# A gated mix of a long convolution and a token MLP: constant transform tables, rows in eights, one more butterfly, and a work order written out as a list

## The chip, the cores and the metric

The kernel runs on one core of a Trainium2 chip. The core has a matrix engine (TensorE, PE in the profile; its weight loads stand as PEld), VectorE (DVE), ScalarE (ACT), GpSimd (POOL) and SyncE (SP), which here only issues DMA transfers. Each engine works through its own queue in order and waits on semaphores. The metric is the device time of one execution in microseconds.

## What is computed

```python
def _A_ref(q, k, v, shift_k, ssm_k, ssm_D):        # q, k, v: [1, 2048, 640]
    k_shift = zeros; for t in range(4):
        k_shift += k_pad[:, t:t + S, :] * shift_k[:, 3 - t]
    kv = k_shift * v
    kv_f = rfft2(kv padded to 4096); kf_f = rfft2(ssm_k padded to 4096)
    y = irfft2(kv_f * kf_f)[:, :S, :].astype(bfloat16)
    return q * (y + kv * ssm_D)

def _B_ref(x, w1, b1, w2, b2):                     # over the tokens
    h = _layernorm(x)                              # over the 640 channels
    u = gelu(einsum("bsd,sf->bdf", h, w1) + b1)    # F = 1536
    return (einsum("bdf,fs->bds", u, w2) + b2).transpose(0, 2, 1)

x = A_q
g = sigmoid((x * gate_w).sum(-1, keepdims=True))
return g * _A_ref(x, ...) + (1 - g) * _B_ref(x, ...)
```

All inputs are bfloat16; S = 2048 tokens, D = 640 channels.

## The kernel before

Everything is held in on-chip memory once loaded. Tokens lie on the 128 partitions, channels along the free axis, in halves of 320 columns per matmul.

**Two strands.** The MLP strand: X (A_q) is loaded in four groups of 512 rows; per tile of 128 tokens VectorE takes `bn_stats` twice and `bn_aggr` once (`ln_tile`), GpSimd makes the reciprocal root (`ln_scale`), VectorE normalises X in place (`ln_apply`). Then 12 x 4 groups of eight matmuls ("m1", X by the w1 chunks in `ring`) with a gelu on ScalarE, and 16 output tiles of 24 matmuls ("m2", GT by W2), each with an eviction on ScalarE into O1. The convolution strand: the ssm kernel is transposed on TensorE (`transp`, tile wT), transformed with cosine and sine tables (`fwd`, `fwd_even`, table FTB, result C), and combined by additions on VectorE (`mixing`); k is reordered (`k_turn`, on VectorE), transposed by DMA, convolved with the four taps on TensorE (`kv`) and multiplied by v; the two halves of kv go through the same transforms; `cross` and `product` multiply the spectra on VectorE, with some sums left to accumulating DMAs from GpSimd's queue; `invmix` makes the additions of the inverse transform, and `inverse` does its matmuls, scales them by the gate on ScalarE ("cg"), multiplies by q and adds to O1 on VectorE, and writes the output. Half 0 of the sequence goes first, half 1 last.

**Tables.** The 4096-point transform is split into four phases p = 0..3 (the rows 4i + p). The table FTB is made in the kernel: GpSimd writes index patterns (`iota` into brow, acol, jrow), VectorE makes index products modulo 4096 (pint), and ScalarE takes the sine, four times. The inverse's table is FTB transposed by four DMA transposes into GTB, then reordered by four ScalarE copies back into FTB ("gil").

**Even phases.** The forward transforms of phases 0 and 2 use half the matmuls and three VectorE additions (`fwd_even`) for all but the first half of the ssm kernel. The inverse uses eight matmuls per output tile for every phase.

**Start.** TensorE runs matmuls on a tile of zeros (`spin`) until the first data is there and between the transposes of ssm: `SPIN = (7, 2, 1, 1, 1)`, and one more ahead of the first transform. SyncE's queue loads ssm block 0, ssm blocks 1 and 2, x0, ssm blocks 3 and 4, x1, x2, x3, the biases, the second half of ssm, w1 and k, in that order.

**What sets the order.** Every step is added once to a planner (`SC.add`, class `_Sched`), with an engine, an estimated duration, what it reads and writes, and a priority. `run` plays these through a model with one queue per engine, four PSUM slots and a DMA model, and emits each engine's instructions in the order found. A tracker (`_Tracker`) then puts the semaphore waits in. Matmul accumulators are taken from four slots of two banks (pp0 to pp3).

```python
SPIN = (7, 2, 1, 1, 1)
LB = [0, 8, 13, 16]                       # tiles per batch of the layernorm's roots
W2S = ((20, 24, 28), (16, 0, 4), (8, 12, 20), (24, 28, 16))
```

Of the kernel before, what the change touches and what calls it, by code (L numbers as in the profile page):

```python
# [313 lines left out]
class _Op:  # L314
    __slots__ = ("eng", "dur", "emit", "prio", "idx", "ndep", "succ", "vt", "vtrole", "end", "start", "kind", "lat", "deps", "name", "after", "nafter", "asucc", "lock")
# [13 lines left out]
class _Sched:  # L329
# [29 lines left out]
    def add(self, eng, dur, emit, reads, writes, prio=None, vt=None, lat=0.0, name=""):  # L359
# [9 lines left out]
        if vt is not None:  # L369
            vt.left += 1  # L370
            if vt.last_pe is not None:
                deps.add(vt.last_pe)
            if eng == "PE":
                if vt.first is None:
                    vt.first = op
                vt.last_pe = op
            else:
                for d in deps:
                    if d.vt is not vt and not vt.keep:
                        if d not in vt.first.deps:  # L380
                            vt.first.deps.add(d)
        op.deps = deps
        op.after = set()
        self._rec(op, reads, "R")
# [4 lines left out]
    def run(self):  # L389
        ops = self.ops  # L390
        for op in ops:
            op.succ = []
            op.asucc = []
            op.ndep = len(op.deps) + len(op.after)
        for op in ops:
            for d in op.deps:
                d.succ.append(op)
            for d in op.after:
                d.asucc.append(op)
        engs = list(ENGS) + ["SP", "QA"]  # L400
        ready = {e: [] for e in engs}
        pend = {e: [] for e in engs}
        free = {"ACT": 2.93, "DVE": 0.85, "POOL": 0.83, "PE": 1.18, "SP": 0.0, "QA": 0.0}
        port = {"DVE": 0.0, "POOL": 0.0}
        dma_free = 0.3
        avail = {}
        for op in ops:
            avail[op] = 0.0
            if op.ndep == 0:
                heapq.heappush(pend[op.eng], (0.0, op.prio, op.idx))  # L410
        nfree = list(range(self.NSLOT))
        held = {}
        events = []
        order = []
        t = 0.0
        done = 0
        started = 0
        n = len(ops)
        frees = []
        while started < n:  # L420
            while frees and frees[0][0] <= t:
                _, sl, cls = heapq.heappop(frees)
                nfree.append(sl)
                held[cls] -= 1
            nxt = []
            progress = False
            for e in engs:
                while pend[e] and pend[e][0][0] <= t:
                    _, p, i = heapq.heappop(pend[e])
                    heapq.heappush(ready[e], (p, i))  # L430
                if free[e] > t:
                    nxt.append(free[e])
                    continue
                skipped = []
                pick = None
                while ready[e]:
                    p, i = heapq.heappop(ready[e])
                    op = ops[i]
                    if op.vt is not None and op.vt.slot is None:
                        c = op.vt.cls  # L440
                        if not nfree or held.get(c, 0) >= self.limit.get(c, 99):
                            skipped.append((p, i))
                            continue
                    pick = op
                    break
                for s in skipped:
                    heapq.heappush(ready[e], s)
                if pick is None:
                    if pend[e]:
                        nxt.append(pend[e][0][0])  # L450
                    continue
                op = pick
                progress = True
                started += 1
                if op.vt is not None and op.vt.slot is None:
                    op.vt.slot = nfree.pop(0)
                    held[op.vt.cls] = held.get(op.vt.cls, 0) + 1
                op.start = t
                if e in ("SP", "QA") or op.lat < 0:
                    issue = 1.2 if e == "POOL" else 0.1  # L460
                    s = max(t + issue, dma_free)
                    dma_free = s + op.dur
                    op.end = dma_free + 2.0 + (6.0 if e == "POOL" else 0.0)
                    free[e] = t + issue
                else:
                    op.end = t + op.dur
                    if op.lock:
                        op.end += max(port["POOL" if e == "DVE" else "DVE"] - t, 0.0)
                        port[e] = op.end
                    free[e] = op.end  # L470
                order.append(op)
                if op.vt is not None:
                    op.vt.left -= 1
                    if op.vt.left == 0:
                        heapq.heappush(frees, (op.end + 0.05, op.vt.slot, op.vt.cls))
                for s in op.asucc:
                    avail[s] = max(avail[s], op.start)
                    s.ndep -= 1
                    if s.ndep == 0:
                        heapq.heappush(pend[s.eng], (avail[s], s.prio, s.idx))  # L480
                for s in op.succ:
                    lat = 0.08 if s.eng == e else 0.15
                    if e == "PE" and s.eng == "PE":
                        lat = 0.0
                    avail[s] = max(avail[s], op.end + lat)
                    s.ndep -= 1
                    if s.ndep == 0:
                        heapq.heappush(pend[s.eng], (avail[s], s.prio, s.idx))
                nxt.append(free[e])
            if not progress:  # L490
                c = [x for x in nxt if x > t]
                if frees:
                    c.append(frees[0][0])
                assert c, "schedule stuck: " + str([(o.name, o.eng, o.ndep) for o in ops if not hasattr(o, "end")][:12])
                t = min(c)
        self.order = order
        self.makespan = max(o.end for o in ops)
        return order
# [6 lines left out]
def bass_gated_mix__ssm_conv_h3__mixer_token_mlp__prompt_kernel(  # L505
    nc, A_q, A_k, A_v, A_shift_k, A_ssm_k, A_ssm_D, B_x, B_w1, B_b1, B_w2, B_b2, gate_w, out
):
    with nc.Block() as blk:

        @blk.tensor  # L510
        def _(pe_engine):
            _build(nc, A_q, A_k, A_v, A_shift_k, A_ssm_k, A_ssm_D, B_x, B_w1, B_b1, B_w2, B_b2, gate_w, out)


def _build(nc, A_q, A_k, A_v, A_shift_k, A_ssm_k, A_ssm_D, B_x, B_w1, B_b1, B_w2, B_b2, gate_w, out):
# [10 lines left out]
    with ExitStack() as es:  # L526
# [48 lines left out]
        gth = alloc("gth", [128, 16], F32)  # L575
# [4 lines left out]
        FTB = alloc("FTB", [128, 4, 2, 2, 2, 128], BF16)  # L580
        GTB = alloc("GTB", [128, 4, 2, 2, 2, 128], BF16)
# [6 lines left out]
        acol = alloc("acol", [128, 1], I32, at=base_of(SS))  # L588
        brow = alloc("brow", [128, 128], I32, at=base_of(SS) + 64)
        prod = alloc("prod", [128, 128], I32, at=base_of(SS) + 64 + 2048)  # L590
        tb = alloc("tb", [128, 2, 2, 128], I16, at=base_of(SS) + 64 + 2560)
# [13 lines left out]
        pint = alloc("pint", [128, 4, 2, 2, 256], I16, at=base_of(ring[1]))  # L605
        jrow = alloc("jrow", [128, 8, 256], I16, at=base_of(ring[1]) + 8192)
# [7 lines left out]
        cgb = [alloc(f"cgb{i}", [128, 2, D], BF16, at=base_of(GTB) + 2560 * i) for i in range(3)]  # L614
# [7 lines left out]
        def dve_dur(n, mode):  # L622
            return n / {1: 960.0, 2: 1920.0, 4: 3840.0}[mode] + (0.04 if mode == 4 else 0.08)

        def act_dur(n, nap=0):
            return n / 1200.0 + 0.09 + 0.05 * nap
# [32 lines left out]
        def act(o, i, func, bias=None, scale=None, acc=None, vt=None, prio=None, name="act"):  # L659
# [17 lines left out]
            return SC.add("ACT", act_dur(n_of(o), nap), emit, rr if vt is not None else rr + [i], ww, prio=prio, vt=vt, name=name)  # L677
# [21 lines left out]
        def mms(vt, items, prio=None, name="mm"):  # L699
            dur = sum(max(n_of(r) / 2400.0 + 0.0025, 0.056) for _, _, r, _, _ in items)  # L700
# [11 lines left out]
        last = [None]  # L712

        def dma(o, i, nbytes, stream="SP", prio=None, sem=None, rate=365.0, chain=False, **kw):
# [7 lines left out]
            if chain:  # L722
                if last[0] is not None:
                    o_.after.add(last[0])
                last[0] = o_
# [14 lines left out]
        def ssm_load(h, a, b):  # L740
            dma(ssm[:, a:b, 1024 * h:1024 * h + 1024], dr(A_ssm_k, 128 * S * a + 1024 * h, [[S, 128], [128 * S, b - a], [1, 1024]]), 128 * (b - a) * 2048, chain=True, rate=({0: 262.0, 1: 223.0}.get(a, RL3)) if h == 0 else 385.0)
# [625 lines left out]
```

## Time and profile before

Three runs took 179.3, 179.79 and 182.12 us, median 179.79. One further execution was profiled; the profile gives its span, 178.7 us from the first instruction to the last, and not its own time.

| engine or queue | busy us | what it does most |
|---|---|---|
| PE | 170.9 | 1104 matmuls of 320 columns, 160 of the taps, 80 transposes |
| DVE | 169.5 | additions and products of the transforms |
| ACT | 117.0 | 64 evictions into C (40.5), 15 into O1 (13.3), 16 of the inverse (12.7) |
| POOL | 43.1 | KF (8.1), index patterns, issue of accumulating DMAs |
| DMA | 43.51 MB | mean 243 GB/s over the span |

The profile's page lists the busy time of each engine, the idle time just before groups of instructions with what ended it, and a chain of waits followed back from the last instruction. A table by stage gives the same busy times for stretches of the span. Rows of the timeline give the start, the length, the engine, the source line, the operation and how many were merged. A row "x3" of several instructions overlaps a little: the start-to-start time of one is a bit below its duration. Line 298 is the helper that issues every matmul, 632 that of every two-input VectorE or GpSimd operation, 676 that of every ScalarE operation, 272 that of every DMA.

### The profile page before, as it was taken

How to read it: one execution, taken by the hardware profiler on the slowest of the kernel's cores; microseconds unless marked ns; L12 is line 12 of the kernel's file. 1: busy time of each engine (PE TensorE's matmuls, PEld its weight loads, DVE VectorE, ACT ScalarE, POOL GpSimd, SP SyncE). 2: the span in 40 equal slices, each digit the busy share in tenths (PEclk: the TensorE clock that was granted, in tenths of full speed). 3: DMA queues.
4: the chain of work that ended last, by engine and by line, in shares of the span. 5: the costliest groups of instructions: out<-in, count | busy, mean ns of one | idle time of the engine just before them, and what ended most of it. 6: DMA issues, size and time to landing. Idle time of an engine off the chain costs nothing.

```text
span 178.7 us, 3326 instructions
## 1 busy us (share of the span) xinstructions
PE 170.9 (96%) x1373; PEld 128.4 (72%) x1374; DVE 169.5 (95%) x203; ACT 117.0 (65%) x176; POOL 43.1 (24%) x52
## 2 busy tenths in 40 slices
PE   7868999899999999999999999999999999999993
PEld 2545787487778677776777778888888887777772
DVE  7799889979999999999999899999999999999984
ACT  4998997999899999428999921131231323753760
POOL 8099803100000065000241100403525000252000
PEclk9999999999999999999999999999999999999999
DMA  5999999999999999999499989797999999599463
GB/s 145 384 413 372 388 301 206 264 421 299 213 258 289 189 272 235 229 229 231 97 244 285 173 132 363 158 229 241 171 194 221 208 201 394 205 164 236 114 233 138
DMA packets 38542, 43.51 MB, mean 243 GB/s; under 512 B 15867, under 2 KB 31360, under 8 KB 38528
## 3 DMA queue, kind: packets, MB, share of 16 engines
q1 hardware_dynamic: 33296, 32.16, 59.1%
q0 software_dynamic: 5200, 11.14, 35.8%
q8 instruction: 11, 0.18, 0.4%
q14 instruction: 3, 0.02, 0.0%
q10 hardware_dynamic: 32, 0.01, 0.0%
HBM read 25.87 MB, written 2.62 MB: 159 GB/s over the span
## 4 chain that ended last, share of the span: by engine, by line
PE 88%; DMA 6%; ACT 3%; SPq 2%; issue 0%; DVE 0%
PE pp L298 88%; DMA rows<-in_B_b_dram 6%; SPq L272 2%; ACT C L676 1%; ACT L676 1%; ACT GT L676 0%; DVE O L688 0%
## 5 line engine op out<-in xcount | busy, mean ns | idle before, releaser
L632 DVE TENSOR_TENSOR C<-C 128x2560 bf16<-128x2560 bf16 (+2 forms) x37 | 54.5, 1525 | 1.1 <-ACT C L676 1.1
L298 PE MATMUL pp<-X,ring 128*128 128x320 bf16 x384 | 55.4, 299 | 0.0
L298 PE MATMUL pp<-GT,W 128*128 128x320 bf16 x384 | 52.6, 299 | 0.0
L298 PEld LDWEIGHTS pp<-GT,W 128*128 128x128 bf16 x384 | 43.6, 114 | 8.6
L298 PEld LDWEIGHTS pp<-X,ring 128*128 128x128 bf16 x384 | 37.3, 98 | 14.3
L676 ACT ACTIVATE C<-pp 128x640 bf16<-128x640 f32 x64 | 40.5, 737 | 3.2 <-PE pp L298 3.2
L676 ACT ACTIVATE O<-pp,c,omg 128x640 bf16<-128x640 f32 x15 | 13.3, 884 | 34.7 <-PE pp L298 34.7
L267 POOL DMA_DIRECT2D C<-C x8 | 11.0, 1615 | 45.0 <-DVE C L632 45.0
L298 PE MATMUL pp<-wT,FTB 128*128 128x320 bf16 x112 | 17.1, 299 | 1.4 <-ACT wT L676 0.8
L676 ACT ACTIVATE cgb<-pp,gg 128x640 bf16<-128x640 f32 x16 | 12.7, 794 | 5.7 <-PE pp L298 5.3
L676 ACT ACTIVATE GT<-pp,cc 128x640 bf16<-128x640 f32 x12 | 9.6, 801 | 9.0 <-PE pp L298 9.0
L298 PEld LDWEIGHTS pp<-wT,FTB 128*128 128x128 bf16 x112 | 10.5, 98 | 6.5 <-ACT wT L676 1.2
L945 DVE BATCH_NORM_STATS2 stats<-X 128x6 f32<-128x320 bf16 x32 | 13.5, 461 | 1.1 <-DMA X<-in_A_q_dram 1.1
L632 DVE TENSOR_TENSOR tm<-C,C 128x2560 bf16<-128x2560 bf16 (+1 forms) x7 | 14.3, 2060 | 0.0
L298 PE MATMUL pp<-C,FTB 128*128 128x320 bf16 x96 | 13.4, 299 | 0.0
L267 POOL DMA_DIRECT2D C<-q_hi x6 | 5.9, 977 | 27.6 <-DVE C L632 13.1
L298 PEld LDWEIGHTS pp<-C,FTB 128*128 128x128 bf16 x96 | 9.3, 98 | 3.8 <-issue 0.2
L676 ACT ACTIVATE gq<-gq 128x640 bf16<-128x640 bf16 x16 | 11.8, 739 | 0.1
L632 DVE TENSOR_TENSOR SS<-C 128x2560 bf16<-128x2560 bf16 x8 | 11.7, 1488 | 0.1
L632 DVE TENSOR_TENSOR C<-tm 128x2560 bf16<-128x2560 bf16 (+1 forms) x9 | 10.7, 1194 | 0.1
L676 ACT ACTIVATE ksh<-pp 128x1024 bf16<-128x1024 f32 (+1 forms) x12 | 9.9, 903 | 0.2 <-PE pp L298 0.2
L676 ACT ACTIVATE wT<-pp 128x1024 bf16<-128x1024 f32 x10 | 9.7, 1027 | 0.6 <-PE pp L298 0.6
(77 smaller groups left out, 188.8 us busy)
## 6 DMA issues: line engine op xcount, KB each, us to landing
ring<-in_B_w_dram SPq DMA_DIRECT2D x12, 512.0 KB, 9.6
W<-in_B_w_dram SPq DMA_DIRECT2D x12, 512.0 KB, 6.3
C<-C POOLq DMA_DIRECT2D x8, 640.0 KB, 10.6
X<-in_A_q_dram SPq DMA_DIRECT2D x4, 640.0 KB, 9.0
kn<-in_A_k_dram SPq DMA_DIRECT2D x4, 640.0 KB, 9.3
out_dram<-O SPq DMA_DIRECT2D x7, 320.0 KB, 3.2
C<-SS POOLq DMA_DIRECT2D x3, 640.0 KB, 11.7
ssm<-in_A_ssm_k_dram SPq DMA_DIRECT2D x3, 512.0 KB, 7.4
```

Source lines behind the costliest of these rows:

```text
L267: ins = engobj.dma_start(out_ap, in_ap, accum_op=ALU.add, max_dma_last_dim=2560)
L272: ins = engobj.dma_start(out_ap, in_ap)
L298: ins = self.nc.tensor.matmul(ps_ap, lhsT=lhsT, rhs=rhs, start=start, stop=stop, skip_group_check=True)
L632: o_ = SC.add(eng, d, lambda s: T.op(eng, lambda e: e.tensor_tensor(o, a, b, op), rd, [o]), rd, [o], prio=prio, name="tt")
L676: return T.op("ACT", lambda e: e.activation(o, src, func, **kw), rr + [src], ww)
L945: ops.append(SC.add("DVE", 0.38, (lambda o, i: lambda s: T.op("DVE", lambda e: e.bn_stats(o, i), [i], [o]))(o, i), [i], [o]))
```

## The change

- **Tables.** The host writes the cosine and sine tables into the program (`_tables`, two inline tensors of 128 x 4096 bf16, 1.05 MB each). FTB is loaded by two DMAs early, GTB by one DMA later. The index patterns, products, sines, the four DMA transposes and the four reorderings go.
- **Rows in eights.** All row groups (X, w1, W2, outputs, the gate and the biases) use rows 8i + j of a half of 1024, as k and v already did, in place of 4i + p of a quarter. The m2 weights are read from W2 with a stride of 8 elements in place of 4. W2 is loaded in 2 x 6 pieces of 2 KB runs in place of 4 x 3 pieces of 1 KB runs.
- **Inverse butterfly.** For half 1 (`INVE = (1,)`), `invmix` makes four more additions of 2 x 640 elements, and phases 0 and 2 of `inverse` take four matmuls per tile in place of eight.
- **Row work.** Of 16 layernorm applications, six run on ScalarE (tiles 4, 7, 8, 11, 12, 14), with a new operand -mean x rstd from GpSimd. `bn_aggr` goes; GpSimd combines the partial statistics with small operations in four batches of four tiles. One of four k reorderings moves to ScalarE, two of ten evictions of wT move to VectorE.
- **Fillers and small loads.** Seven zero matmuls at the start, none later. The biases are loaded from ScalarE's queue. A gelu on one column right at the start loads ScalarE's table.
- **Order.** `run` is replaced by `follow`, which emits the 728 steps in the order of a list and takes the PSUM slots from a string.

```diff
-    def run(self):
+    def follow(self, order, slots):
...
+        for vt, s in zip(vts.values(), slots):
+            vt.slot = s
+        self.order = [self.ops[i] for i in order]
...
+        ftab, gtab = (nc.inline_tensor(a, name=n).ap() for a, n in zip(_tables(FALL, GALL), ("ftab", "gtab")))
...
-        SPIN = (7, 2, 1, 1, 1)
+        NSPIN = 7
+        SPIN = (0, 0, 0, 0, 0)
...
-        iota(brow[:, :], [[4, 128]], 1, 0)
-        iota(acol[:, :], [[0, 1]], 0, 8)
...
-            sins[p] = act(FTB[:, p, :, :, :, :].rearrange("q a b c d -> q (a b c d)"), pa, ACT.Sin, bias=cst[:, 0:1],
-                scale=-(2.0 * math.pi / 4096.0) * (1.0 - 1e-6), name="sin")
...
+            if a // 4 in BNP:
+
+                mq, m2 = V(stats, 12 * a + 1, [[12, n], [3, 4]]), V(stats, 12 * a + 2, [[12, n], [3, 4]])
+                dq, me = V(dev, 4 * a, [[4, n], [1, 4]]), V(mv, 2 * a, [[2, n], [0, 4]])
+
+                def red(o, h, off, s1, s4):
+                    tt("POOL", V(gth, 2 * a, [[2, n], [1, 2]]), V(h, off, [[s1, n], [s4, 2]]), V(h, off + 2 * s4, [[s1, n], [s4, 2]]), ALU.add, prio=0)
+                    tt("POOL", o, V(gth, 2 * a, [[2, n]]), V(gth, 2 * a + 1, [[2, n]]), ALU.add, prio=0)
+                red(gpre[:, a:b], stats, 12 * a + 1, 12, 3)
+                ts("POOL", mv[:, a:b, 0], gpre[:, a:b], 0.25, None, ALU.mult, prio=0)
+                tt("POOL", dq, mq, me, ALU.subtract, prio=0)
+                tt("POOL", dq, dq, dq, ALU.mult, prio=0)
+                ts("POOL", dq, dq, 160.0, None, ALU.mult, prio=0)
+                tt("POOL", dq, dq, m2, ALU.add, prio=0)
+                red(gpre[:, a:b], dev, 4 * a, 4, 1)
+                ts("POOL", sd[:, a:b], gpre[:, a:b], 1.0 / D, 1e-5, ALU.mult, ALU.add, prio=0)
...
+                    o_ = act(xs, xs, ACT.Identity, bias=nm[:, t:t + 1], scale=rstd[:, t:t + 1], prio=1, name="lna")
...
-            gtbs.append(dma(GTB[:, p, :, :, :, :].rearrange("q a b c d -> q (a b c) d"), FTB[:, p, :, :, :, :].rearrange("q a b c d -> q (a b c) d"), 128 * 2048, rate=200.0, transpose=True, chain=True))
+        dma(GTB[:, :], dr(gtab, 0, [[NGT, 128], [1, NGT]]), 256 * NGT, tok="g")
...
+            if g in INVE:
+                tt("DVE", q4(ha, sa, 0, 1), q4(ha, sa + 1, 0, 2), q4(ha, sa + 1, 1, 2), ALU.add)
+                tt("DVE", q4(ha, sa, 2, 1), q4(ha, sa + 1, 0, 2), q4(ha, sa + 1, 1, 2), ALU.subtract)
+                tt("DVE", q4(hb, sb, 0, 3), q4(hb, sb + 1, 0, 2), q4(hb, sb + 1, 3, -2), ALU.subtract)
+                tt("DVE", q4(hb, sb, 1, 1), q4(hb, sb + 1, 2, -2), q4(hb, sb + 1, 1, 2), ALU.add)
...
+                    else:
                         for c in range(2):
                             for ci in range(2):
-                                items.append((chk(ci), V(FTB, 1024 * p + 512 * c + 256 * k2 + 128 * kt, [[1, 128]]), V(hz, sz * SL + (2 * c + k2) * D + 320 * ci, [[1, 320]]),
-                                              k2 == 0 and c == 0, k2 == 1 and c == 1))
+                                items.append((chk(ci), gtb(p, c, 0, kt), V(hz, sz * SL + (2 * kt + c) * D + 320 * ci, [[1, 320]]), c == 0, c == 1))
...
-        SC.run()
+        SC.follow([int(i) for i in _ORDER.split()], [int(i) for i in _SLOTS])
```

The list holds the numbers of the steps in the order in which the code adds them, so each engine's new queue can be counted out. SyncE's begins: ssm blocks 0 and 1, ssm blocks 2 to 4, x0, the first half of the table, x1, its second half, x3, the second half of ssm in two parts, x2, k1, w1, k0, then the DMA transposes of k1 and k0 and the rest of w1, k and v. TensorE's: the seven fillers, the taps' constants, ssm blocks 0, 1, 4, 2, the bias constants, block 3, eleven groups of the first transform mixed over the phases, the second half's transposes, the remaining groups mixed with the even phases of the second half; the first m1 group comes after all sixteen groups of the first half and one odd-phase group of the second. VectorE's: the statistics of tiles 0 to 7 and 12 to 15, two evictions of wT, the statistics of tiles 8 to 11 with the reordering of k1 among them, four applications, and the reordering of k0. Products and additions that depend on each other stand further apart than before.

## The prediction

> **What bounds the kernel now.** I read the page's shares first, then busy time by stage (cut where the chain of waits changes), then the chain itself.
>
> ```profile
> span 178.7 us, 3326 instructions
> PE 170.9 (96%) x1373; PEld 128.4 (72%) x1374; DVE 169.5 (95%) x203; ACT 117.0 (65%) x176; POOL 43.1 (24%) x52
> 0.00:14.82 14.82, 10.63 (x76) 5.76 (x78) 12.69 (x42) 11.82 (x13) 9.47 (x20) 1.00 0.87 321
> 14.82:35.92 21.10, 20.20 (x169) 14.76 (x170) 19.65 (x48) 19.24 (x29) 9.16 (x12) 1.00 1.10 302
> 35.92:106.20 70.28, 70.28 (x616) 52.01 (x617) 68.18 (x63) 59.13 (x103) 10.28 (x10) 1.00 1.00 236
> 106.20:149.70 43.50, 43.50 (x323) 36.32 (x321) 43.12 (x28) 12.29 (x14) 9.39 (x8) 1.00 0.99 229
> 149.70:176.03 26.33, 26.32 (x193) 19.59 (x191) 25.26 (x25) 14.47 (x18) 4.80 (x4) 1.00 0.76 210
> 35.92 140.11 PE pp L298 x1128
> 176.06 0.55 DVE O L688
> ```
>
> The stage columns are stage and length, then busy time of PE, weight loads, DVE, ACT and POOL, granted clock, DMA share, GB/s. TensorE loses 14.82 - 10.63 = 4.19 us in the first stage and 0.90 in the second, nothing from 35.92 to 176.03, and 2.67 us of finish and output follow: 170.93 + 5.10 + 2.67 = 178.7. The chain agrees: 140.11 us of matmuls in one piece. But VectorE is nearly as full: of its 169.5 us, 6.1 lie before its first statistic at 8.28; the other 163.4 stand in the 168.3 us to its end at 176.6. So an edit pays only if both engines' accounts shrink. DMA is full in the first two stages too.
>
> The span is 178.7 us; the median of the runs is 179.79. The profiled execution's own time isn't listed, so I add the difference, 1.1 us, to every span.
>
> **The change part by part.** *Inverse butterfly.* For the second half of the sequence, phases 0 and 2 need 4 matmuls per output tile in place of 8: 2 phases x 2 tiles x 4 = 16 fewer. 320 matmuls of the second product fill 43.63 us, 136 ns each: TensorE -2.2 us. VectorE gets four additions of 1280 elements; that row takes 0.82 us alone, 0.74 from start to start: +3.0 us.
>
> *Fillers.* 13 matmuls on zeros become 7. The 12 recorded took 4.9 us, the first seven 3.16: -1.8 us of busy time, but in the head, where it turns into idle time unless something moves forward.
>
> *Tables.* VectorE loses 0.29 + 0.31 + 0.30 + 4 x 0.68 + 4 x 0.43 = 5.4 us, all before 8.28, where its first statistic waits for x:
>
> ```profile
> 8.28 1.28 DVE L945 BATCH_NORM_STATS2 stats<-X 128x6 f32<-128x320 bf16 x3 [1.08 <-DMA X<-in_A_q_dram]
> 9.63 0.72 PE L298 MATMUL pp<-ident,ssm 128*128 128x128 bf16 x8 [0.85 <-DMA ssm<-in_A_ssm_k_dram]
> 6.31 0.72 PE L298 MATMUL pp<-ident,ssm 128*128 128x128 bf16 x8 [0.58 <-DMA ssm<-in_A_ssm_k_dram]
> 51.67 9.97 SPq L265 DMA_TRANSPOSE GTB<-FTB  x4
> ```
>
> So that saving is worth nothing by itself. ACT loses four sines (4.5 us) and four reorderings (5.1); SyncE's queue loses the four transposes (9.97 us), with the next weights behind them, which TensorE doesn't wait for today. The price is a table of 1.05 MB among the first loads, another later. The three waits above end when 0.79, 1.44 and 1.97 MB of the queue have landed: 391 KB/us at the end, so 2.7 us for the first table, on whatever is queued behind it. With the new order (counted out from the list's numbers: two ssm loads, x0, table part 1, x1, table part 2, x3, ssm's second half, x2, k1, w, k0) the same line gives: ssm 5.5 and 7.8, x0 9.6, table 11.0, x1 12.6, table 14.0, x3 15.7, ssm 17.7 and 19.0, x2 20.7, k1 22.4, k0 25.4. The k transposes wait on that queue for VectorE's two reorderings of k (24.4 and 28.2 by its list below) and hold it 3.7 us each (7.36 for two), until 31.9; three w loads, k2, k3, v0 and v1 stand behind them. The first of these w is read at 35.0. It lands between 34.7 (2.8 us, the quickest ssm row, 256 KB) and 37.3 (5.4, v); I take 35.4, 2.8 and 0.65 for the other 256 KB: 0.4 us of TensorE.
>
> *Head on TensorE and ACT.* The kernel's five transposes can't finish before 7.8; ACT evicts them at 0.94 us each, until 11.2. TensorE starts the W transforms at 11.4 (now 12.47), and the 1.0 us wait for the b rows at 14.8 goes, since they move to ACT's queue. Then ACT is the pace: 0.605 us per eviction (14 in 8.45) against 0.54 for four matmuls. Eleven evictions and the small one end at 18.9, three wT at 21.7, nineteen more at 33.1. By then TensorE has done 26.6 us of the list (fillers 3.0; transposes 6.7, five of 0.8 with D's row and five of 0.55; constants 0.6; 22 groups of 0.54, eight of 0.27, two of 1.09) at about 33.3: 6.7 us idle, with the 0.4 above 7.1, against 5.1 now. From there matmuls are on hand as now.
>
> *Row work.* Per tile, two statistics and the aggregate take 0.855 us, without it 0.75: -1.7. Six of 16 applications go to ACT (-6 x 0.36), one k reordering too (-0.74). Two wT evictions come to VectorE; no row shows that shape, it lies between 0.55 (320 from PSUM) and 3 x 0.55, and I take 1.15 each, in step with the element count: +2.3. With the butterflies VectorE's path work is 163.4 - 1.7 - 2.2 - 0.7 + 2.3 + 3.0 = 164.1, and it starts at 9.6 in place of 8.28. ACT's new work (6 x 0.8, between its 640-element rows of 0.74 and 0.88, and 2.4 for the reordering from 0.739 per 640) stands after 33 us, where its row is 59.13 of 70.28 and loses 5.1; nothing if it's hidden there, 7 us at worst.
>
> The Trainium skill, "ScalarE: Activation LUTs", section "Rules for kernel authors", speaks against this: add and multiply belong on VectorE, up to about three times faster. By that rule the six applications alone would cost 2.6 us more than they do now and the change would be 2.6 us slower for it; the page's shares (VectorE 95%, ACT 65%) make it a gain of 2.2 on the engine that is full.
>
> *Statistics on GpSimd.* The aggregate becomes fourteen POOL operations per four tiles, in one fixed queue. Nearest rows:
>
> ```profile
> 20.09 0.33 POOL L632 TENSOR_TENSOR sd<-sd,rstd 128x8 f32<-128x8 f32 x1
> 28.29 0.32 POOL L646 TENSOR_SCALAR sd<-mv 128x3 f32<-128x3 f32 x1 [6.18 <-DVE mv L949]
> 28.70 0.92 POOL L632 TENSOR_TENSOR rstd<-sd,cst 128x3 f32<-128x3 f32 x1
> ```
>
> The second operation of tiles 4 to 7 can't start before their statistics, at 16.3. From it to the last reciprocal root there are 43 small operations and 4 powers. VectorE wants that root at 33.2: it starts at 9.6 and has 23.6 us ahead of it (32 statistics of 0.42, two evictions 2.3, two reorderings 1.5, six applications 2.1, additions of 2.9 and 1.4). At 0.10 us (the start-to-start of the smallest iotas) and 1 us per power they end at 24.6; at 0.41 (28.29 to 28.70, dependent) and 1.44 per power at 39.7, a stall of 6.5 us. I take 0.27, the mean of the three products in this shape, because the list interleaves independent groups, and 1.1 per power: 16.3 + 11.6 + 4.4 = 32.3, price 0. The cover is 0.9 us thin, and each 0.1 us more per operation is 4.3 us.
>
> *Rows in eights.* Weights of the second product are read with stride 8 in place of 4. The ssm transposes have that stride: 40 loads of 147 ns in 2.8 us, one per 70 ns, below the 136 ns of a matmul: 0. If a load took its whole 147, 384 x 11 ns = +4.2.
>
> *End.* The two final operations come behind the last matmul, in the order 1, 0; now one runs before it: +0.5, a finish of 3.2.
>
> **Sum.** TensorE: 170.9 - 2.2 - 1.8 = 166.9 busy, 7.1 idle, 3.2 finish: 177.2, +1.1 = 178.3. VectorE: 9.6 + 164.1 + 1.2 (its waits; 4.9 now, of which 2.4 are for loads and the first mixing) + 2.1 output = 177.0, +1.1 = 178.1. The accounts meet at 178, 1% below now, and I forecast 178.0.
>
> Clock: gaps of 1.4 us and less replace fillers, and the page grants full clock throughout; I charge nothing. The skill's "TensorE: Matmul & The Clock Gate", section "Why this matters for your kernels", allows idle gaps up to about 3 us. By its half rate for a window of 3.4 us a cold spell would add an estimated 1.7 us.
>
> **Rivals.** *The head is no longer than now* (0.33): the first loads come half a microsecond earlier and ACT's pace is hidden. Idle between 3.2 (fillers end at 4.3 as now, 1.2 before them, 2 at ssm's waits) and 5.1 as now, finish 2.7: 166.9 + 4.6 + 2.7 + 1.1 = 175.3, 173.9 at best. For it: 1.1 us earlier W start, no wait at 14.8. Against: ACT is 19.24 of 21.10 in the second stage already.
>
> *GpSimd's queue sets the pace* (0.12): at 0.41 per operation VectorE stands still for 6.5 us at its last applications, and TensorE waits for normalised X in its fixed order: 178 + 6.5 = 184.5. With powers of 1.44 it is slower by 2% (183.4) from 0.38 on. For it: dependent start-to-start of 0.41; against: 0.31 from 20.09 to the next one.
>
> *The stride costs* (0.02): a load every 147 ns in place of 136 gives 178 + 4.2 = 182.2; against it stand the 70 ns.
>
> **Numbers.** Forecast (0.53): 178, its own range 176 to 182.5, the upper part for the stride, ACT and the middle prices of GpSimd. The range for 8 in 10 takes in the fast rival to its best, 173.9 to 182.5; about 1 in 10 lies outside on each side. Within 2% (176.2 to 183.4) is what a measurement here can't tell from no change: faster 0.35 (the first rival and the forecast's lowest edge), same 0.52, slower 0.13.
>
> **What would show it.** W transforms starting near 11.4; 16 fewer 320-column matmuls; TensorE idle about 7 us before 36 and none after; the last power on POOL near 32 and VectorE not waiting for it; weight loads of 147 ns with matmuls still 136 ns apart; 0.5 us more after the last matmul. Wrong if TensorE or VectorE has gaps of microseconds after 40 us: the fixed order, not the head, would then be the story.

## The result, and the profile after

The changed kernel takes 190.07 us (median of 4, 188.37 to 191.67); the kernel before took 180.16 beside it (179.3 to 182.12). The ratio is 1.0516 with a 95% interval of 1.0442 to 1.0591: slower by about 5%. The forecast was 178.0, with a range to 182.5. The profiled execution's own time is 188.37, its span 186.5, so 1.87 us lie outside the span. In this and all later results an execution more than 1.5% above the quickest of its kernel is left out of the ratio and its interval, but not of the median beside it.

The first view is the page's shares and its clock row (tenths of full speed, 40 slices of 4.7 us):

```profile
span 186.5 us, 3295 instructions
PE 172.3 (92%) x1356; PEld 134.8 (72%) x1356; DVE 165.9 (89%) x174; ACT 111.3 (60%) x173; POOL 69.1 (37%) x89
PEclk9999999999999999999759999999999999999999
```

VectorE is 3.6 us less busy than before, as meant; TensorE is busier by 1.4 us although it runs fewer matmuls. The clock row shows why there is more to find: it falls to 7 and 5 tenths in the middle. Busy time by stage (stage and length, then PE, weight loads, VectorE, ACT, POOL, clock, DMA share, GB/s) puts the place:

```profile
0.00:15.00 15.00, 12.13 (x99) 7.76 (x100) 7.88 (x23) 9.56 (x14) 9.43 (x14) 1.00 0.87 317
15.00:36.00 21.00, 18.76 (x166) 11.95 (x163) 17.45 (x33) 20.09 (x32) 18.24 (x50) 1.00 0.99 283
36.00:60.00 24.00, 23.04 (x240) 17.74 (x240) 23.93 (x19) 22.01 (x28) 5.47 (x5) 1.00 0.91 267
80.00:90.00 10.00, 7.91 (x59) 5.48 (x56) 4.03 (x6) 4.46 (x11) 5.21 (x4) 1.00 0.72 124
90.00:100.00 10.00, 7.32 (x37) 4.56 (x38) 9.31 (x10) 5.87 (x10) 1.19 (x1) 0.66 1.06 307
110.00:150.00 40.00, 40.00 (x295) 37.93 (x293) 39.76 (x29) 9.17 (x14) 10.25 (x9) 1.00 0.85 201
```

The head is near the forecast: TensorE idles 2.87 + 2.24 us before 36 (about 7 were forecast), and 0.96 from there to 60 (none was forecast). The loss is between 80 and 100 us: 59 + 37 matmuls, where a stretch of the same work without the loss has 150 (shown below). 54 matmuls at 136 ns are 7.3 us. VectorE works only 4.03 us from 80 to 90. The chain of waits there (start, length, what) names who was late, and the timeline of GpSimd (start, length, engine, line, operation, count, idle time before) shows the instruction:

```profile
69.87 11.69 POOL nm L559
81.56 5.87 DMA C<-C
...
87.52 0.83 DVE q_hi L559
...
92.68 90.64 PE pp L298 x644
```

```profile
68.45 1.42 POOL L267 DMA_DIRECT2D C<-SS  x1 [26.97 <-DVE C L559]
69.46 12.15 POOL L559 TENSOR_TENSOR nm<-nm,rstd 128x4 f32<-128x4 f32 x1
81.56 2.42 POOL L267 DMA_DIRECT2D C<-C  x2
83.04 2.17 POOL L267 DMA_DIRECT2D C<-SS  x1
```

A product of 128x4 numbers takes 12.15 us; the same operation on the other three groups of tiles takes 0.20 us each, at 24.3, 33.7 and 35.5 us. It finishes the negated, scaled row means of tiles 0 to 3, which only ScalarE's applications read, and those four tiles are applied on VectorE: nobody reads its result. Three accumulating DMAs of the value mixing stand behind it on GpSimd's queue. VectorE's and TensorE's timelines show the price:

```profile
80.00 1.56 DVE L559 TENSOR_TENSOR gq<-X,gwb 128x1280 bf16<-128x1280 bf16 x2
87.52 0.83 DVE L559 TENSOR_TENSOR q_hi<-C,C 128x1280 bf16<-128x1280 bf16 x1 [5.97 <-DMA C<-C]
```

```profile
92.68 2.31 PE L298 MATMUL pp<-kv,FTB 128*128 128x320 bf16 x8 [4.77 <-ACT C L603]
94.79 2.34 PE L298 MATMUL pp<-X,ring 128*128 128x320 bf16 x8
```

VectorE runs gapless until 81.56, and in that moment the product ends. Then VectorE stands for 5.97 us, until the mixed sums have landed; TensorE idles 4.77 us and then runs eight matmuls in 2.3 us, half speed.

### The profile page after: what moved, and what is told of

The parts are those of the page before. It is cut to its first block, busy times and chain, and to the rows that moved or that the text cites. A ratio compares the mean times of both kernels' runs of the same rounds, so it can differ in the third digit from the quotient of the medians.

```text
span 186.5 us, 3295 instructions
## 1 busy us (share of the span) xinstructions
PE 172.3 (92%) x1356; PEld 134.8 (72%) x1356; DVE 165.9 (89%) x174; ACT 111.3 (60%) x173; POOL 69.1 (37%) x89
## 4 chain that ended last, share of the span: by engine, by line
PE 54%; DVE 14%; POOL 12%; DMA 11%; SPq 3%; issue 3%; ACT 0%; DVEq 0%
PE pp L298 54%; DMA kn<-in_A_k_dram 8%; DVE C L559 7%; POOL nm L559 6%; SPq L272 3%; DMA C<-C 3%; DVE SS L559 2%; DVE kv L559 2%; POOL rstd L559 1%; POOL dev L559 1%; POOL nm L573 1%; POOL gth L559 1%; DVE stats L881 1%; DVE X L574 1%; POOL C L267 1%
## 5 line engine op out<-in xcount | busy, mean ns | idle before, releaser
L559 DVE TENSOR_TENSOR C<-C 128x2560 bf16<-128x2560 bf16 (+2 forms) x41 | 58.0, 1454 | 1.0 <-ACT C L603 0.7
L298 PE MATMUL pp<-X,ring 128*128 128x320 bf16 x384 | 58.2, 303 | 0.7 <-DVE X L574 0.6
L298 PE MATMUL pp<-GT,W 128*128 128x320 bf16 x384 | 54.6, 300 | 0.0
L298 PEld LDWEIGHTS pp<-GT,W 128*128 128x128 bf16 x384 | 51.9, 144 | 1.3 <-ACT O L603 0.4
L267 POOL DMA_DIRECT2D C<-SS x3 | 4.8, 1596 | 34.7 <-DVE C L559 34.7
L298 PEld LDWEIGHTS pp<-wT,FTB 128*128 128x128 bf16 x112 | 9.7, 97 | 9.4 <-ACT C L603 3.6
L267 POOL DMA_DIRECT2D O<-q_hi x4 | 4.8, 1325 | 27.3 <-DVE q_hi L559 27.3
L298 PE MATMUL pp<-kv,FTB 128*128 128x320 bf16 x48 | 9.7, 335 | 4.8 <-ACT C L603 4.8
L559 POOL TENSOR_TENSOR nm<-nm,rstd 128x4 f32<-128x4 f32 x4 | 12.7, 3187 | 0.2
L298 PE MATMUL pp<-C,GTB 128*128 128x320 bf16 x80 | 12.0, 299 | 0.0
```

The lines of the kernel that those rows point to most:

```text
L267: ins = engobj.dma_start(out_ap, in_ap, accum_op=ALU.add, max_dma_last_dim=2560)
L298: ins = self.nc.tensor.matmul(ps_ap, lhsT=lhsT, rhs=rhs, start=start, stop=stop, skip_group_check=True)
L559: o_ = SC.add(eng, d, lambda s: T.op(eng, lambda e: e.tensor_tensor(o, a, b, op), rd, [o]), rd, [o], prio=prio, name="tt")
```

## The experiments

**The theory and its rivals.** The theory: GpSimd's product reads SBUF, and VectorE's string of additions and products with two tensor inputs keeps it out; what stands behind it on GpSimd's queue waits too. Rivals: the new fixed order asks for the sums too early, wherever the product stands; or any GpSimd instruction is slow at that place.

*Move the product.* One number of the fixed order moves; on GpSimd's queue that is:

```diff
-nm = -mean (tiles 0-3) ... KT copy, mixing DMA 2, nm * rstd (tiles 0-3), mixing DMAs 1, 0, 3
+nm = -mean (tiles 0-3), nm * rstd (tiles 0-3) ... KT copy, mixing DMAs 2, 1, 0, 3
```

> The changed kernel with one entry of its fixed order moved: the 128x4 product that finishes the row means of tiles 0 to 3 stands directly behind the subtraction that feeds it, ahead of all four accumulating DMAs of the value mixing, and no longer between the second and the third issued. Theory (a GpSimd operation that reads SBUF waits out VectorE's gapless two-input operations, and the DMAs behind it wait with it): that operation takes under 1 us, the idle of TensorE at 88 to 93 us and the half clock behind it vanish, 10 us go, 177 to 180 us. Rival (the new fixed order asks for the mixed values too early, wherever that operation stands): the gap stays within 2 us of its size, 186 us or more. A result between, 181 to 185 us, would mean both.

183.41 us, ratio 1.0221 (1.0142 to 1.03). In the timeline of GpSimd the product is now at 35.95 us and takes 0.24, and the stages of the hole are full:

```profile
80.00:90.00 10.00, 10.00 (x75) 7.00 (x73) 10.00 (x11) 7.76 (x17) 0.00 (x0) 1.00 0.97 232
90.00:100.00 10.00, 10.00 (x75) 7.17 (x73) 10.00 (x13) 4.47 (x10) 4.15 (x4) 1.00 1.06 266
```

The idle time and the half clock are gone with one entry moved, so the order as a whole isn't what made them. The time is 3.4 us above the expected upper end, in the stretch that was to mean that both theory and rival have a share; that rest is taken up below.

*Replace it where it stands.*

```diff
-            nms.append(tt("POOL", nm[:, a:b], nm[:, a:b], rstd[:, a:b], ALU.mult, prio=0))
+            if a == 0:
+                nms.append(memset("POOL", nm[:, a:b], 0.0, prio=0))
+            else:
+                nms.append(tt("POOL", nm[:, a:b], nm[:, a:b], rstd[:, a:b], ALU.mult, prio=0))
```

> The changed kernel with its order as it is; in the place of the 128x4 product between the accumulating DMAs stands a memset of the same 128x4 tile (its result is read by nobody: tiles 0 to 3 are normalised without it). Theory (the wait is for a read of SBUF beside VectorE): the memset takes 0.3 us or less at about 69.5 us, and the time is that of the kernel with the product moved, 177 to 180 us. Rival (any GpSimd instruction behind the issue of an accumulating DMA, or beside VectorE's string, is slow): the memset takes some 12 us in the product's place, 188 to 191 us.

181.98 us, ratio 1.0102 (1.0058 to 1.0146). GpSimd's timeline:

```profile
71.92 0.56 POOL L628 MEMSET nm<- 128x4 f32 x1
71.97 2.92 POOL L267 DMA_DIRECT2D C<-C  x2
```

And VectorE's:

```profile
71.27 2.81 DVE L559 TENSOR_TENSOR C<-C 128x5120 bf16<-128x5120 bf16 x1
```

A GpSimd instruction in the same place that writes the same tile and reads nothing takes 0.56 us: more than the 0.3 expected, but it ends inside one two-input instruction of VectorE. The time is 2 us above the expected upper end. So neither the place behind a DMA nor VectorE's work as such is slow; the read is what waits.

*Put one into the kernel before* (its neighbours on GpSimd's queue stand in words; VectorE, ScalarE, GpSimd and TensorE do the rest in the same order as before).

```diff
 first accumulating DMA of the value mixing
+small_ = tt("POOL", dmy[:, :], rstd[:, 0:4], rstd[:, 0:4], ALU.mult, prio=0)
 second, third and fourth accumulating DMA
```

> The kernel before with one operation added: a 128x4 f32 product on GpSimd into a tile that nobody reads, between the first and the second accumulating DMA of the value mixing; nothing else of the change is in it. Theory: the product starts near 64 us and is held until VectorE first stands still, at least 5 us; the DMAs behind it land that much later, VectorE runs dry and the time is 183 to 195 us. Rival (the hole belongs to the change's new order): the product takes under 1.5 us and the time is within 1 us of the kernel before.

189.55 us, ratio 1.0539 (1.0487 to 1.0592): one instruction of 512 numbers, read by nobody, costs the kernel before 9.5 us, about as much as the whole change. GpSimd's timeline in the kernel before without it:

```profile
63.19 2.68 POOL L267 DMA_DIRECT2D C<-C  x2 [27.11 <-DVE C L632]
68.78 2.43 POOL L267 DMA_DIRECT2D C<-SS  x2 [2.91 <-DVE C L632]
```

The timelines of GpSimd and of VectorE with it:

```profile
62.89 1.42 POOL L267 DMA_DIRECT2D C<-C  x1 [26.77 <-DVE C L632]
63.91 21.89 POOL L632 TENSOR_TENSOR dmy<-rstd 128x4 f32<-128x4 f32 x1
85.74 1.21 POOL L267 DMA_DIRECT2D C<-C  x1
```

```profile
84.92 0.82 DVE L632 TENSOR_TENSOR gq<-X,gwb 128x1280 bf16<-128x1280 bf16 x1
85.66 0.23 DVE L646 TENSOR_SCALAR gpre<-mv,gws 128x16 f32<-128x16 f32 x1
85.80 1.48 DVE L632 TENSOR_TENSOR tm<-C,C 128x2560 bf16<-128x2560 bf16 x1
```

The product is held for 21.89 us, past sixteen VectorE instructions, each of which begins before the one ahead of it has ended. It ends at 85.80, and VectorE had no idle time there: it had begun a small f32 operation with one tensor input. The expectation had it held until VectorE first stands still. That made a sharper form of the theory, and the next run.

*Add an instruction to VectorE.* The changed kernel as it is, the product in its bad place, and a one-input operation of 128x4 in VectorE's string:

```diff
+        dmy = alloc("dmy", [128, 4], F32)
+        ts("DVE", dmy[:, :], V(cst, 1, [[0, 4]]), 2.0, None, ALU.mult)
```

> The changed kernel, its order untouched, the 128x4 product still between the accumulating DMAs; added is one VectorE operation of 128x4 f32 with one tensor input (a constant times 2 into a tile that nobody reads), behind the 5120-element addition at 68.8 to 71.6 us, in the middle of VectorE's string. Theory, sharpened by the kernel before with a small product (held until exactly such a small one-input f32 operation began on VectorE, 85.66 to 85.80 us, with no idle time around it): GpSimd gets in at any VectorE operation that reads one small input, so the product takes about 2 us in place of 12 and the time falls to 181 to 184 us, although an instruction was added. Rival (GpSimd gets in only when VectorE stands still): the product still takes 11 to 12.5 us, time 188 to 191 us.

182.68 us, ratio 1.0124 (1.0059 to 1.0189). VectorE's and GpSimd's timelines:

```profile
70.64 0.17 DVE L573 TENSOR_SCALAR dmy<-cst 128x4 f32<-128x4 f32 x1
70.72 0.81 DVE L559 TENSOR_TENSOR gq<-X,gwb 128x1280 bf16<-128x1280 bf16 x1
```

```profile
68.58 2.21 POOL L559 TENSOR_TENSOR nm<-nm,rstd 128x4 f32<-128x4 f32 x1
70.73 2.42 POOL L267 DMA_DIRECT2D C<-C  x2
```

The product ends with the new operation, after 2.21 us instead of 12.15, and an added instruction takes 7.4 us off the median. Where the theory of an idle VectorE would have left 12 us, GpSimd got in without any idle time.

That a VectorE instruction has one input isn't enough, though. In the changed kernel's head a small GpSimd operation was held past a bf16 copy and an addition, until VectorE had nothing to do; GpSimd's timeline, then VectorE's:

```profile
26.31 1.74 POOL L573 TENSOR_SCALAR nm<-mv 128x4 f32<-128x4 f32 x1
```

```profile
26.42 0.82 DVE L694 COPY kp<-kn 128x2560 bf16<-128x2560 bf16 x1
27.16 0.82 DVE L559 TENSOR_TENSOR C<-C 128x1280 bf16<-128x1280 bf16 x1
28.28 1.49 DVE L559 TENSOR_TENSOR C<-C 128x2560 bf16<-128x2560 bf16 x1 [0.30 <-ACT C L603]
```

The copy has one tensor input and didn't let GpSimd in. The bf16 type alone isn't it either: beside the scalings of X just before (bf16, 25.01 to 26.51 us) three GpSimd operations took 0.27 to 0.33. What sets the copy apart from the operations that let GpSimd in, no run here shows.

The Trainium skill, "SBUF — State Buffer", section "Who interferes with whom", says that a VectorE instruction with two SBUF inputs contends with a GpSimd instruction that reads SBUF, not with one that only writes it, and that the one that comes first keeps the shared pair of ports for its whole instruction. The 12.15 us against the memset's 0.56 agree with the kind. The length goes further than the page: the wait isn't for one instruction (the longest here is 2.82 us) but for ten, and for sixteen in the run above.

**What is left without the hole.** The three repaired kernels stay at 182.0 to 183.4 us, 1 to 2% above the kernel before. These runs are about that rest.

*Undo the inverse butterfly* (`INVE = (1,)` to `INVE = ()`, on the kernel with the memset, the end of the order laid out anew):

> The changed kernel with the memset in the product's place (182.0 us), and the inverse butterfly undone: 16 more matmuls of 320 columns (+2.2 us of TensorE), four additions fewer on VectorE (-3.0 us). If TensorE sets the end, as in the sum of the prediction: +2.2, 184.2 us. If the outputs at the end are late for VectorE's additions: 180 us or less. If it is neither (both engines have slack there): within 0.7 us of 182.0.

185.04 us, ratio 1.0173 (1.0112 to 1.0235). TensorE is busy for 172.6 us, against 170.5 in the kernel with the product moved: +2.1, the term of the sum. Between the same two profiles, whose heads are alike, the last matmul starts 2.3 us later (178.19 against 175.87) and the span ends 1.2 us later. By the ratios the time went up by 1.3 us, less than the 2.2 expected, and the intervals overlap. That speaks for TensorE setting the end and for the butterfly earning its matmuls, but doesn't prove it.

*Aggregate tiles 8 to 15 on VectorE* (`BNP = (0, 1, 2, 3)` to `(0, 1)`):

> The changed kernel with the memset in the product's place (182.0 us), and the variances of tiles 8 to 15 aggregated on VectorE again, as before the change: eight VectorE operations of about 0.1 us more, eighteen small GpSimd operations fewer. Theory: the two waits of VectorE for GpSimd's roots at 31.3 and 35.3 us (0.93 and 1.80 us) mostly go, because GpSimd's queue gets ahead of VectorE's mixing additions; TensorE's idle time before 45 us falls by 1 to 2 us and so does the time: 180 to 181 us. Rival (those waits are covered by other late work in the head): within 0.5 us of 182.0.

184.87 us, ratio 1.0173 (1.0079 to 1.0268): no gain, and by the ratios 1.3 us above the kernel with the memset, outside the rival's bound too, though the intervals overlap. VectorE's two waits for the roots are gone from the profile, and eighteen fewer GpSimd operations bought nothing. That fits what the rival said, that other late work in the head covers those waits.

*Exchange the two last operations* (on top of that):

> As the run with aggregation of tiles 8 to 15 on VectorE, and the two last operations of VectorE exchanged, so that the one whose matmuls end first goes first, as before the change: 0.3 to 0.6 us less than that run, by the step of the prediction that charged 0.5 us for it; if the end is set by the output transfers, no difference.

182.66 us, ratio 1.0127 (1.0085 to 1.017). The two medians differ by more than the edit could give, but their intervals overlap, and in the profiles 4.2 us pass from the last matmul's start to the end of the span in both. No difference there, as expected if output transfers set the end. The busy times of the last stage say the same, first of the kernel before, then of the one with the added operation:

```profile
176.00:178.00 2.00, 0.02 (x1) 0.00 (x0) 0.55 (x1) 0.00 (x0) 0.00 (x0) 1.00 0.39 140
```

```profile
176.00:178.00 2.00, 0.00 (x0) 0.00 (x0) 0.35 (x1) 0.00 (x0) 0.00 (x0) 1.00 1.01 355
```

Before, the queues move 140 GB/s after the last matmul, with a DMA share of 0.39; now 355, with a share of 1.01.

*The head's clock.* The profiles show a second thing that repaired kernels don't share. TensorE's timeline in the changed kernel, and then in the one with the memset:

```profile
7.08 0.71 PE L298 MATMUL pp<-ident,ssm 128*128 128x128 bf16 x8
...
11.03 6.16 PE L298 MATMUL pp<-wT,FTB 128*128 128x320 bf16 x43 [0.58 <-ACT wT L603]
```

```profile
8.00 1.07 PE L298 MATMUL pp<-ident,ssm 128*128 128x128 bf16 x8
...
13.16 7.00 PE L298 MATMUL pp<-wT,FTB 128*128 128x320 bf16 x33 [0.85 <-ACT wT L603]
```

The same eight transposes take 0.71 us in one and 1.07 in the other, and the long row of W transforms starts 2.1 us later and runs slower. The clock row of the page says 9 for both: it shows nothing before the clock's first record, and the durations must be read instead. Of nine profiles with seven fillers up front and none behind, four were like the second; these four executions took 184.75 to 185.52 us, where the quickest of the same kernels took 181.81 to 182.40. The next kernels copy k where the changed kernel transposes it on the way, so they compute the convolution on other data; they are compared among themselves. First their base:

> A base for the three kernels beside it: the changed kernel with the memset in the product's place (182.0 us), in which the four transposing transfers of k are plain copies of the same bytes, so the convolution works on k that isn't transposed; only times within these four kernels are compared. SyncE's queue is held some 3 us less by each copy, so the head should be no longer: 178 to 182 us; the runs in two groups some 3 us apart, if the fillers' theory below holds.

183.22 us, ratio 1.0148 (1.0092 to 1.0204), above the 178 to 182 expected.

*Stronger fillers* (the fillers' tile is also cleared first):

```diff
-        NSPIN = 7
-        SPIN = (0, 0, 0, 0, 0)
+        NSPIN = 8
+        SPIN = (0, 1, 1, 1, 1)
```

> As the base with plain copies of k, and the fillers of the head strengthened: VectorE clears the fillers' tile first (they start some 0.7 us earlier), eight of them stand up front in place of seven and one ahead of four of the five groups of transposes, twelve in all, one fewer than before the change. In the profiled run of the changed kernel with the memset the granted clock is first recorded as full 17.8 us into the span and eight transposes take 1.07 us; in the changed kernel's 5.4 us and 0.71 us. Theory (with seven fillers TensorE's clock opens by luck, early or 12 us late, 3 us of the head): full clock before 9 us, W transforms 136 ns apart from their start, the runs within 1.5 us of each other, the median at the base's faster group or up to 0.5 us above. Rival (the late clock has another cause): runs 3 us above the others as in the base, or the profile cold until 17 us.

183.18 us, ratio 1.0111 (1.0051 to 1.0172): a miss. The profile isn't cold until 17 us any more, but W transforms are 267 ns apart from 12 to 15 us: the fillers push the transposes back, TensorE then waits 0.98 us for ScalarE's last eviction, and a stretch at half clock follows. In this profile the cold spell was moved, not removed. In the two kernels that follow, with the same fillers and the same wait, the row of W transforms starts at 12.17 and 13.67 us and runs at full speed, 43 in 6.16 us; so the stretch doesn't come in each execution.

*Outputs earlier* (the first two gated products ahead of two additions of the inverse mixing):

> As the run with stronger fillers and copies of k, and the first two gated products of the first half of the sequence, with their accumulating transfers, moved ahead of two additions of the inverse mixing that nothing waits for yet. Theory (the change's order lets the outputs leave too late: in the run with the one-input operation the DMA share is 1.01 from 176 us to 178 us and 4.2 us pass from the last matmul's start to the end of the span, 3.0 before): two outputs leave 2 to 4 us earlier, that last stretch falls to 3.0 to 3.5 us, the time by 0.7 to 1.2 us. Rival (the last stretch is only the two last operations and one transfer): no difference within 0.4 us.

183.81 us, ratio 1.02 (1.0147 to 1.0253). The last stretch fell from 4.2 to 3.6 us, a little short of what was expected, but the time didn't fall: TensorE waited 0.96 us at 168.1 and 0.48 at 169.6 for VectorE, ahead of it. VectorE's timeline shows that the edit wasn't free, since q isn't there yet:

```profile
160.77 0.82 DVE L557 TENSOR_TENSOR q_hi<-cgb,q_hi 128x1280 bf16<-128x1280 bf16 x1 [1.87 <-DMA q_hi<-in_A_q_dram]
```

*And aggregation on VectorE again*:

> As the run with moved outputs and copies of k, and the variances of tiles 8 to 15 aggregated on VectorE again. Theory (in a head with the clock open, VectorE's two waits for GpSimd's roots, 0.93 and 1.80 us, stand on the path): 0.7 to 1.5 us less than the run without it. Rival (TensorE is short of other things there, loads and evictions): within 0.4 us.

183.61 us, ratio 1.0181 (1.0129 to 1.0233), within 0.2 us of the run without it: the rival, for the second time.

*Load q's first half first* (on the base; the order of four loads on SyncE's queue):

> As the base with plain copies of k (183.2 us, its undisturbed runs 181.9 to 183.3), with one change on SyncE's queue: the two loads of q's first half stand ahead of the two of its second half, as before the change; in the changed kernel one load of the second half stands first and waits for its buffer. Theory (that load holds the queue: q_hi is loaded at 152 us, before the change at 142.8): q_hi is issued before 146 us; alone it moves the outputs little, since VectorE's order stands: 0 to 0.7 us less than the base, and TensorE's gaps between 155 and 170 us (1.36 us at 164 in the base) gone. Rival (something else holds q back, or nothing waits for it): issue still near 150 us, or no difference in the gaps.

182.52 us, ratio 1.0159 (1.0116 to 1.0203). SyncE's queue:

```profile
151.90 1.64 SPq L270 DMA_DIRECT2D q_hi<-in_A_q_dram  x2
```

The loads go out at 151.9, not before 146: the theory of the queue holds in part. In the base's profile they go out at 153.76, straight behind q_lo's load, for which SyncE's queue has waited 22.4 us (an accumulating DMA ends that wait). Here the queue waits 17.3 us, for an addition of VectorE's that ends at 151.87. The profile of the kernel with the memset, whose head is as slow as this one's, has them at 155.75. So the load ahead held q_hi for some 2 to 4 us, and behind it that addition does. TensorE's gap at 164 us was gone in this profile, but it is missing in the one with stronger fillers too, which has the old order of loads; so it isn't shown to be the edit's doing.

*Outputs earlier, with that order and fillers up front alone* (eight, their tile cleared first):

> As the run with q's first half loaded first, and the first two gated products with their accumulating transfers moved ahead of two additions; the fillers' tile is cleared first and eight fillers stand up front, none between the transposes. Theory: with q there, the outputs leave 3 us earlier, from the last matmul's start to the end 3.0 to 3.5 us in place of 4.2, no wait of VectorE for q_hi: its quickest runs at 179.5 to 181 us, 1 to 2 us below the base's quickest (181.9). Rival (the last stretch isn't set by the outputs' start): within 0.5 us of the base.

182.79 us, ratio 1.0141 (1.0097 to 1.0185): 0.4 us below the base, and VectorE's wait for q_hi is gone. The last stretch is 3.6 us, and the quickest execution took 181.15, 0.7 us below the base's quickest: between what the theory asked (1 to 2) and what the rival allows (0.5).

*With fillers between the transposes too*:

> As the run before it in this list, with a filler ahead of four of the five groups of transposes too (twelve in all). If fillers between the transposes buy a clock that opens in each run, its runs lie closer together and its median is lower, by up to 1 us; if they only delay the transposes, as the first run with them suggested (a half-clock window 12 to 15 us into the span), its median is 0.5 to 1 us higher than without them.

181.85 us, ratio 1.0094 (1.0062 to 1.0126), the lowest of these seven kernels: 1.4 us below the base by the medians, 1.0 by the ratios, whose intervals overlap. The executions don't lie closer together (180.82 to 184.73, against 181.15 to 183.72 without these fillers), so a clock that opens in each one isn't shown. No kernel of the study is quicker than the one before.

## Why the prediction was wrong

**The step that failed** is "Statistics on GpSimd", with its "price 0". I counted 43 small operations and four powers "to the last reciprocal root" and stopped there, because VectorE wants nothing later from them. But "fourteen POOL operations per four tiles, in one fixed queue" have operations behind the root, and one of them stood between accumulating DMAs that VectorE's products wait for. I hadn't followed that queue to its end, nor asked who waits behind each entry. What the runs put in its place: the product was held for 12.15 us, and that cost 7.3 us by the missing matmuls, 7.4 by the medians with and without the one-input operation.

**The price of an operation** was taken from rows where VectorE happened not to exclude GpSimd. 0.27 us was no bad mean there: the changed kernel's rows are 0.19 to 0.27 while VectorE does statistics. Beside VectorE's two-input strings the same operations take 1.3 to 12.15, so no single price existed, and the bounds 0.10 to 0.41 didn't hold the cost. The skill's rule on the shared ports, cited above, speaks against this change, and I weighed two other rules.

**The rival "GpSimd's queue sets the pace"** had the right engine and the wrong place and mechanism: the last power ended at 35.45 us (forecast 32.3) and VectorE did wait for roots, 0.93 us until 31.45 and 1.80 until 35.49, but taking that away changed nothing clear of the noise, twice. Its sum of 184.5 was for that wait. The prediction's last sentence named the true sign, gaps of microseconds after 40 us, as what would overturn it; it got no rival of its own and no price.

**What held.** The inverse butterfly: 80 matmuls in place of 96 on that row, +2.1 us of TensorE when it was undone, -2.2 forecast. ScalarE's new work: 0.93 us per application (0.8 forecast; VectorE takes 0.44) and 2.34 for the reordering (2.4). The stride: weight loads of 144 ns and matmuls still 136 apart, price 0. W transforms at 11.03 (forecast 11.4). Idle time before 36: 5.1 us (forecast about 7). That TensorE sets the end without the hole is supported by the run without the butterfly, not proved.

**The sum without the hole.** The profile with the one-input operation has a span of 179.2 and a time of 181.09, against 178.3 forecast. TensorE ends at 175.3 in place of 174.0: 169.9 busy and 5.4 idle, where I had 166.9 and 7.1. Waits too short to show as idle time stand in that busy time, since a matmul counts as 299 ns and the next can start after 136. The finish is 3.9 in place of 3.2, for the outputs. Between span and time lie 1.9 us, and I had taken 1.1 from the difference between a span and a median of other executions. 1.3 + 0.7 + 0.8 = 2.8: 181.1. The median is 1.6 higher; a head at half clock in some executions would give that, as four of nine profiles have it and lie some 3 us above the quickest of their kernels, but it isn't shown for the executions of this kernel that weren't profiled.

**Clock.** "I charge nothing" failed twice. The 4.77 us gap was followed by a stage at 0.66 of the full clock, and seven fillers didn't open the clock in each execution. The Trainium skill, "TensorE: Matmul & The Clock Gate", section "Why this matters for your kernels", allows gaps up to about 3 us; the gap of 4.77 agrees, and the smaller waits at 36 to 60 us left the clock at 1.00. In the head that bound wasn't enough: in three of the five profiles with eight fillers a wait of only 0.83 to 0.98 us ahead of the W transforms was followed by some 3 us of matmuls 267 ns apart.

**What stays open.** Why the addition of VectorE's that q_hi's load waits for comes at 152 us, where the kernel before loads q_hi at 143; and how the last 1% is shared between head and outputs. A kernel with the hole closed, the transposes kept and all of the later edits wasn't run.

## What to carry to other kernels

Follow every operation that moves to a queue to the end of that queue: an operation that nobody reads is not free when somebody waits for what stands behind it. Don't put a GpSimd operation that reads SBUF ahead of DMAs on GpSimd's queue while VectorE runs strings of two-input operations; put it before the string, make it a write only, or break the string with a small one-input f32 operation of the kind that did it here. A price for a small GpSimd operation is worth only as much as the row's neighbours on VectorE.

## What the runs showed of the hardware

The wait of GpSimd for VectorE lasts past instruction ends, as long as the next two-input instruction follows without a gap: 12.15 us past ten, 21.89 us past sixteen. One f32 operation of 128x4 (0.17 us) or 128x16 (0.23 us) with one tensor input ended it without any idle time of VectorE; a bf16 copy of 128x2560 with one input (0.82 us) didn't. And the clock row of a page can read 9 where matmuls run at half speed: eight transposes of 1.07 us in place of 0.71 showed it.
